# Eleven pairs of token tiles instead of eight by seven products, in a fused attention and ELU feed-forward kernel

## The chip, the cores and the metric

The kernel runs on one core of a Trainium2 chip. The metric is the device time of one execution in microseconds (us). The engines are TensorE (PE; its weight loads are shown apart as PEld), VectorE (DVE), ScalarE (ACT), GpSimd (POOL) and SyncE (SP), each with a queue of its own that is worked off in order. SP issues output DMAs and transposing DMAs; POOL issues input DMAs.

## The reference

Attention with a causal window of 128 and a linear bias by head, on 8 batches of 8 heads, 576 positions and 64 dimensions, and behind it a feed-forward layer with ELU. All arrays are float32; the kernel multiplies in float16.

```
def _attn_ref(q, k, v):                       # (8, 8, 576, 64) each
    scores = scale * np.matmul(q, k.transpose(0, 1, 3, 2))
    ...
    mask = (rel >= 0) & (rel < window)        # window = 128
    scores = np.where(mask, scores + bias[None], -1000000000.0)
    attn = softmax(scores)
    return np.matmul(attn, v)

def _moe_ref(x, w_in, w_out):                 # x (4608, 512), w_in (512, 2048), w_out (2048, 512)
    h = x @ w_in
    g = np.where(h > 0.0, h, np.exp(np.minimum(h, 0.0)) - 1.0)
    return g @ w_out
```

`x` is the attention's output with the heads of a token side by side: 8 x 576 = 4608 tokens of 512 numbers.

## The kernel before

The order of all work is written out by hand, in steps that the code calls `s` and this text calls slots, from 0 to 152. In most slots PE does one `hidden` group, a piece of `x @ w_in` for 512 outputs per partition (line 300): either 128 tokens and four blocks of 128 hidden channels (16 matmuls of 128 columns, and 32 of 64 columns for some), or from slot 70 on 256 tokens and two blocks (8 matmuls of 256 columns). Two PSUM banks, `hp0` and `hp1`, take turns, so the group of slot s+2 needs the bank that the group of slot s filled.

Behind a hidden group comes the ELU. In a common slot ACT takes exp of the bank (line 310), POOL cuts it at 1 (line 311), and DVE forms max(e - 1, h) from it and the bank and writes it to `g` in float16 (line 318, function `elu`). In a slot of the set `SOFT`, ACT does two passes instead, relu of -h and exp of minus that (lines 307 and 308), and POOL nothing. The elu of slot s-1 is issued behind the hidden group of slot s.

Ahead of it the attention of batches 2 to 7 is spread over 17 slots a batch. Each batch has four units of four slots. In the first slot of a unit PE computes scores (line 225). In the next two, ACT does two exps each (line 231), ahead of its work for the hidden group, and DVE weighs the result with the bias table (line 236). In the fourth, PE multiplies by the values (line 266) and DVE divides (lines 271 and 272). SP then transposes the result to `xT` by DMA (line 280). `turn_qk` transposes blocks of q and k of the next batch on DVE (line 145). Batches 0 and 1 are done in slots 0 to 32 in a form with more PE transposes; batch 1's last units lie in slots 22 to 32, with PE products with the values, DVE reciprocals and products (lines 254 and 255), weighing (line 216) and ACT exps of 1024 columns (line 205).

The second product, `g @ w_out`, is done for pairs of 128-token tiles, numbered n from 0 to 17; pair n belongs to about the slots 15 + 8n to 22 + 8n. There are two ways.

- Standard (`output`, line 324): per tile 16 matmuls of 512 columns into one bank, four in a slot. Even tiles use `op`, odd ones `av`. ACT copies the bank to `ob` (line 331), SP sends it out.
- Seven products, for the pairs in `SEVEN`: the 256 tokens, the 2048 channels and the 512 outputs are each halved, and instead of eight block products there are seven, as in Winograd's form of Strassen's algorithm. Seven products of 8 matmuls with 256 columns, in the order 1, 6, 2, 7, 5, 4, 3, seven matmuls a slot (`product`, line 392). They need sums of blocks of `g` (`sums`: S1 to S4, on DVE, from two slots ahead of the pair to its fourth slot) and of `w_out` (`quarters`: T1 to T4, eight DVE instructions once in the kernel). DVE puts the parts together (`combine`: U2, U3, C22, C21, C12); ACT copies product 1 and the sum of 1 and 2 (lines 395 and 397). All DVE adds of these show as line 348.

The products lie in two banks, x and y (`places`): 1, 2 and then 3 and 5 in x, 6, 7 and 4 in y. For a pair behind a standard one x is `av`, for a pair behind a seven-product one x is `op`. T1 to T3 lie in `s1`, which before slot 25 holds staged q and k of batch 1. Of the pairs with seven products, 5, 7, 9, 11 and 13 have attention beside them; 15, 16 and 17 lie behind the last batch's attention, or at its end.

The six slots from two ahead of a seven-product pair on are soft, and so are slots 40 to 48 (the quarters lie in slots 41 to 48), and the end. The last pair, 17, has no hidden groups beside it; it uses banks of its own, is not spread over slots, and its product 4 is done in two pieces of 128 columns, each with its add and its DMA.

```
        SEVEN = (17, 5, 7, 9, 11, 13, 15, 16)
...
        turns = [(i, j) for i in (1, 6, 2, 7, 5, 4, 3) for j in range(8)]
...
                for d, i, j in ((-2, 1, (0, m)), (-1, 1, (m, 8)), (0, 2, ()), (1, 3, ()), (3, 4, ())):
                    at(s + d, sums, n, i, *j)
                for d, what in ((2, "U2"), (4, "U3"), (5, "C22"), (6, "C21"), (7, "C12")):
                    after(s + d, combine, n, what)
```

Of the kernel before, what the change touches and what calls it, by code (L numbers as in the profile page):

```python
# [18 lines left out]
def kernel(  # L19
# [9 lines left out]
    nc = tc.nc  # L29
    B, H, S, D = q.shape  # L30
    NTOK, DO = out.shape
    FF = moe_w_in.shape[1]
    NFC = FF // 128
    NTB = NTOK // 512
# [39 lines left out]
    sp = [spa[:, 0, :], spa[:, 1, :]] + [ps_s.tile([128, 512], F32, name=f"sp{i}", tag=f"sp{i}") for i in (2, 3)]  # L74
    hp = [ps_h.tile([128, 512], F32, name=f"hp{i}", tag=f"hp{i}") for i in range(2)]
    av = ps_v.tile([128, 512], F32, name="av", tag="av")
    op = ps_o.tile([128, 512], F32, name="op", tag="op")
# [71 lines left out]
    with tc.manual_schedule():  # L149
# [142 lines left out]
        def hidden(t, c0, w, f0, nf, p, soft):  # L292
            hps[t, c0, f0] = p
            a = (512 * t + c0) % RING
            cuts = [(0, w, a)] if a + w <= RING else [(0, RING - a, a), (RING - a, w, 0)]
            for l in range(nf):
                fc = f0 + l
                for u0, u1, x0 in cuts:
                    for c in range(4):
                        nc.tensor.matmul(  # L300
                            p[:, l * w + u0:l * w + u1], w_in_sb[:, c, fc * 128:(fc + 1) * 128],
                            xT[:, c, x0:x0 + u1 - u0], start=(c == 0), stop=(c == 3))
            e = es[t, c0, f0] = work.tile([128, 512], F32, name="e", tag="e", bufs=6)
            n = w * nf
            if soft:

                nc.scalar.activation(e[:, 0:n], p[:, 0:n], AF.Relu, scale=-1.0)  # L307
                nc.scalar.activation(e[:, 0:n], e[:, 0:n], AF.Exp, scale=-1.0)  # L308
                return
            nc.scalar.activation(e[:, 0:n], p[:, 0:n], AF.Exp)  # L310
            nc.gpsimd.tensor_scalar(out=e[:, 0:n], in0=e[:, 0:n], scalar1=1.0, scalar2=0.0,  # L311
                                    op0=ALU.min, op1=ALU.max)
# [30 lines left out]
        def A(n, i, k):  # L343
            c = 256 * (n % 2) + 128 * i
            return gs[n // 2][:, 8 * k:8 * k + 8, c:c + 128]

        def add(o, a, b, op=ALU.add):
            V.tensor_tensor(out=o, in0=a, in1=b, op=op)  # L348
# [6 lines left out]
        SS, U, obs = {}, {}, {}  # L355
# [9 lines left out]
        def places(n):  # L365


            x, y = (op, av) if n - 1 in SEVEN else (av, op)
            return ((x, 0), (y, 0), (x, 256), (y, 256)) if n < 2 * NTB - 1 else (
                (sp[2], 0), (sp[3], 0), (sp[0], 0), (hp[0], 0))  # L370

        def place(n, i):
            o, c = places(n)[(0, 0, 2, 3, 2, 1, 1)[i - 1]]
            return o[:, c:c + 256]

        def kept(n, i):
            if (n, i) not in U:
                U[n, i] = work.tile([128, 256], F32, name=f"U{i}", tag=f"U{i}", bufs=1)
            return U[n, i]

        def tile_out(n, i):
            if (n, i) not in obs:
                obs[n, i] = work.tile([128, DO], F32, name="ob", tag="ob")
            return obs[n, i]

        def product(n, i, j0=0, j1=8, o=None, c0=0, c1=256):
            a, b = {1: lambda: (A(n, 0, 0), WB(0, 0)), 2: lambda: (A(n, 0, 1), WB(1, 0)), 3: lambda: (SS[n, 4], WB(1, 1)),
                    4: lambda: (A(n, 1, 1), T[4]), 5: lambda: (SS[n, 1], T[1]), 6: lambda: (SS[n, 2], T[2]),
                    7: lambda: (SS[n, 3], T[3])}[i]()
            o = place(n, i) if o is None else o  # L390
            for j in range(j0, j1):
                nc.tensor.matmul(o[:, 0:c1 - c0], a[:, j, :], b[:, j, c0:c1], start=j == 0 and i in (1, 4, 5, 6),  # L392
                                 stop=j == 7, skip_group_check=True)
            if j1 == 8 and (i == 1 or i == 5 and n == 2 * NTB - 1):
                nc.scalar.copy(kept(n, i), o)
            if j1 == 8 and i == 2:
                nc.scalar.copy(tile_out(n, 0)[:, 0:256], o)

        def combine(n, what):
            if what == "U2":  # L400
                add(kept(n, 2), kept(n, 1), place(n, 6))
            elif what == "U3":
                add(kept(n, 3), kept(n, 1), place(n, 7))
            elif what == "C22":
                add(tile_out(n, 1)[:, 256:512], kept(n, 3), kept(n, 5) if (n, 5) in U else place(n, 5))
            elif what == "C12":
                add(tile_out(n, 0)[:, 256:512], kept(n, 2), place(n, 3))
                put(n, 0, 0, DO)
            else:
                add(tile_out(n, 1)[:, 0:256], kept(n, 3), place(n, 4))  # L410
                put(n, 1, 0, DO)

        def put(n, i, c0, c1):
            r = 256 * n + 128 * i
            nc.sync.dma_start(out[r:r + 128, c0:c1], tile_out(n, i)[:, c0:c1])

        def last_piece(n, o, c0, c1, e):
            product(n, 4, 0, 8, o, c0, c1)
            add(tile_out(n, 1)[:, c0:c1], kept(n, 3)[:, c0:c1], o[:, 0:c1 - c0])
            put(n, 1, c0, e)  # L420

        wz = one([128, 256], F16, "wz")

# [69 lines left out]
        early, tasks, late, HID, OUT = {}, {}, {}, {}, {}  # L493

        def at(s, f, *a):
            tasks.setdefault(s, []).append((f, a))

        def after(s, f, *a):
            late.setdefault(s, []).append((f, a))
# [14 lines left out]
        for t in range(2, NTB):  # L514
            for j in range(16):
                step = (128 * (j // 4), 128, 4 * (j % 4), 4) if t < 4 else (256 * (j // 8), 256, 2 * (j % 8), 2)
                HID[16 * t + 6 + j] = [(t, *step, BUF[(j + 1) % 2])]
        SEVEN = (17, 5, 7, 9, 11, 13, 15, 16)
        for o in range(16 * NTB):
            t, ts, f = o // 16, o // 4 % 4, o % 4  # L520
            if o // 8 in SEVEN:
                continue
            s = (9, 11, 13, 14)[o] if o < 4 else 11 + o if o < 13 else 2 * o - 1 if o < 16 else 15 + o
            OUT[s] = [(output, (t, ts, 4 * f, (op, op, sp[3], op)[ts] if t == 0 else (op, av)[ts % 2]))]

        def done(r):
            for step in HID[r]:
# [66 lines left out]
        for b in range(2, B):  # L594
            for u in range(4):
                a = START[b] + 4 * u
# [11 lines left out]
            a = START[b - 1] if b > 2 else 0  # L608
            for n in range(4):
                piece = (b, int(n < 2), n % 2)  # L610
                if b == 2:
                    m = 4 if n < 2 else 6
# [8 lines left out]


        for m in range(8):
            at(41 + m, quarters, 1 + m // 2, m % 2)
        turns = [(i, j) for i in (1, 6, 2, 7, 5, 4, 3) for j in range(8)]
        for n in SEVEN:
            s = 15 + 8 * n
            if n < 2 * NTB - 1:
                m = 6 if n >= 8 else 4
# [4 lines that stand above are left out]
                for d in range(8):  # L634
                    OUT[s + d] = [(product, (n, i, j, j + 1)) for i, j in turns[7 * d:7 * d + 7]]
            else:
                at(s - 3, sums, n, 3)
                for i in (1, 2):
                    at(s - 2, sums, n, i, 0, 6)
                    at(s - 1, sums, n, i, 6, 8)  # L640
                at(s - 1, product, n, 1)
                OUT[s] = [(product, (n, 2)), (product, (n, 6)), (combine, (n, "U2")), (sums, (n, 4))]
                OUT[s + 1] = [(product, (n, 5)), (product, (n, 7)), (combine, (n, "U3"))]
                OUT[s + 2] = [(product, (n, 3)), (combine, (n, "C12")), (combine, (n, "C22")),
                              (last_piece, (n, hp[0], 128, 256, DO)), (last_piece, (n, hp[1], 0, 128, 128))]


        SOFT = {s for n in SEVEN for s in range(13 + 8 * n, 19 + 8 * n)} | set(range(40, 49)) | set(range(16 * NTB - 10, 16 * NTB + 8))

        slots = set(HID) | set(OUT) | set(tasks) | set(early)  # L650
        for s in range(min(slots), max(slots) + 1):
            for f, a in early.get(s, []):
                f(*a)
            for step in HID.get(s, []):
                hidden(*step, s in SOFT)
            if s - 1 in HID and s not in (1, 4, 5):
# [37 lines left out]
```

## Time and profile before

| | |
|---|---|
| median of 8 runs | 316.58 us (315.68 to 317.21) |
| profiled execution | 316.05 us, span 314.3 us |
| PE, DVE, ACT, POOL busy | 98%, 75%, 66%, 43% of the span |
| granted TensorE clock | 1.0 |
| hidden groups (L300) on PE | 144.9 us |
| standard products (L324), op and av | 45.2 and 32.8 us |
| elu on DVE (L318) | 138 x 0.684 us in the records |
| relu and exp on ACT in soft slots (L307, L308) | 56 x 0.598 and 0.631 us |
| exp on ACT in common slots (L310) | 87 x 0.60 us |

The span runs from the first to the last instruction; the execution's own time has 1.75 us around it. The chain of waits in a profile is followed back from the last instruction. In the rows of the timeline the first figure is the start in us, the second the length; a length holds the pipeline's run-out, so the next instruction of the engine can start before it is over. A row of busy times by stretch gives the stretch and its length, then busy time and number of instructions of PE, PEld, DVE, ACT and POOL, the granted clock, and the DMA engines' share and rate.

### The profile page before, as it was taken

How to read it: one execution, taken by the hardware profiler on the slowest of the kernel's cores; microseconds unless marked ns; L12 is line 12 of the kernel's file. 1: busy time of each engine (PE TensorE's matmuls, PEld its weight loads, DVE VectorE, ACT ScalarE, POOL GpSimd, SP SyncE). 2: the span in 40 equal slices, each digit the busy share in tenths (PEclk: the TensorE clock that was granted, in tenths of full speed). 3: DMA queues.
4: the chain of work that ended last, by engine and by line, in shares of the span. 5: the costliest groups of instructions: out<-in, count | busy, mean ns of one | idle time of the engine just before them, and what ended most of it. 6: DMA issues, size and time to landing. Idle time of an engine off the chain costs nothing.

```text
span 314.3 us, 9840 instructions
## 1 busy us (share of the span) xinstructions
PE 306.8 (98%) x4119; PEld 238.1 (76%) x4119; DVE 236.2 (75%) x458; ACT 208.1 (66%) x376; POOL 135.1 (43%) x207
## 2 busy tenths in 40 slices
PE   8899999999999999999999999999999999999994
PEld 6788874887777678976787688767877787678884
DVE  4747656787689978886897689778977688577883
ACT  4676458666678668647965787558754875678760
POOL 8947879473780071465256533672233013300000
PEclk9999999999999999999999999999999999999999
DMA  9999999995999259495949891999232102120102
GB/s 99 176 199 202 199 182 165 141 116 68 94 132 134 61 69 132 51 162 75 116 50 165 104 125 24 160 130 118 27 86 54 42 19 86 50 61 2 67 35 101
DMA packets 96364, 32.03 MB, mean 102 GB/s; under 512 B 83904, under 2 KB 91840, under 8 KB 96320
## 3 DMA queue, kind: packets, MB, share of 16 engines
q0 software_dynamic: 75920, 18.36, 64.3%
q1 hardware_dynamic: 20400, 13.05, 16.9%
q8 instruction: 32, 0.52, 0.7%
q14 instruction: 12, 0.10, 0.1%
HBM read 36.70 MB, written 9.44 MB: 147 GB/s over the span
## 4 chain that ended last, share of the span: by engine, by line
PE 90%; DVE 4%; ACT 2%; issue 2%; POOL 1%; ACTq 0%; DVEq 0%; POOLq 0%
PE hp L300 37%; PE op L324 12%; PE av L324 8%; PE av L392 7%; PE op L392 6%; PE spa L225 4%; PE spa L266 3%; PE op L426 2%; DVE g L318 1%; PE sp L248 1%; PE sp L324 1%; PE sp L300 1%; PE sp L392 1%; ACT EX L231 1%; PE spa L176 1%
## 5 line engine op out<-in xcount | busy, mean ns | idle before, releaser
L300 PE MATMUL hp<-xT,wi 128*128 128x128 f16 (+2 forms) x1744 | 144.9, 233 | 0.7 <-DVE g L318 0.3
L300 PEld LDWEIGHTS <-wi 128*128 128x128 f16 x1856 | 124.4, 98 | 26.6 <-issue 5.7
L318 DVE SCALAR_TENSOR_TENSOR g<-e,hp 128x512 f16<-128x512 f32 x138 | 94.4, 684 | 35.3 <-POOL e L311 26.3
L311 POOL TENSOR_SCALAR e<-e 128x512 f32<-128x512 f32 x88 | 55.5, 631 | 136.7 <-ACT e L310 136.2
L310 ACT ACTIVATE e<-hp 128x512 f32<-128x512 f32 x82 | 49.2, 599 | 47.6 <-PE hp L300 44.1
L307 ACT ACTIVATE e<-hp 128x512 f32<-128x512 f32 x56 | 33.5, 598 | 19.2 <-PE hp L300 16.6
L324 PE MATMUL op<-wo,g 128*128 128x512 f16 x176 | 45.2, 379 | 0.0
L236 DVE TENSOR_TENSOR EX<-EX,TAB 128x1024 f16<-128x1024 f16 x48 | 33.1, 690 | 14.9 <-ACT EX L231 14.8
L324 PEld LDWEIGHTS <-g 128*128 128x128 f16 x320 | 27.7, 97 | 20.6 <-issue 1.1
L308 ACT ACTIVATE e<-e 128x512 f32<-128x512 f32 x56 | 35.3, 631 | 1.8
L114 POOL DMA_DIRECT2D VP<-in_v_dram x40 | 34.5, 873 | 0.7 <-DVE xn L255 0.5
L231 ACT ACTIVATE EX<-spa 128x512 f16<-128x512 f32 x48 | 26.1, 595 | 11.1 <-PE spa L225 10.2
L324 PE MATMUL av<-wo,g 128*128 128x512 f16 x128 | 32.8, 379 | 0.0
L392 PEld LDWEIGHTS <-S 128*128 128x128 f16 x256 | 24.2, 98 | 3.4 <-DVE S L348 0.6
L231 ACT ACTIVATE EX<-sp 128x512 f16<-128x512 f32 x48 | 26.0, 598 | 0.0
L392 PEld LDWEIGHTS <-g 128*128 128x128 f16 x200 | 18.7, 98 | 3.0 <-issue 1.0
L272 DVE TENSOR_TENSOR xn<-spa,rden 128x512 f16<-128x512 f32 x24 | 16.6, 692 | 0.8
L108 POOL DMA_DIRECT2D st<-in_k_dram x24 | 16.4, 684 | 0.4 <-issue 0.3
L108 POOL DMA_DIRECT2D st<-in_q_dram x24 | 16.2, 678 | 0.2 <-DMA VP<-in_v_dram 0.2
L392 PE MATMUL op<-s,S 128*128 128x256 f16 x104 | 15.6, 273 | 0.2 <-DVE S L348 0.2
L225 PEld LDWEIGHTS <-KT 32*128 32x128 f16 x480 | 9.0, 92 | 8.5 <-issue 8.0
L225 PE MATMUL spa<-QT,KT 32*128 32x256 f16 (+2 forms) x240 | 15.1, 250 | 0.0
(144 smaller groups left out, 347.6 us busy)
## 6 DMA issues: line engine op xcount, KB each, us to landing
out_dram<-ob SPq DMA_DIRECT2D x35, 256.0 KB, 2.2
VP<-in_v_dram POOLq DMA_DIRECT2D x32, 128.0 KB, 5.1
st<-in_k_dram POOLq DMA_DIRECT2D x24, 144.0 KB, 4.3
st<-in_q_dram POOLq DMA_DIRECT2D x24, 144.0 KB, 4.2
wi<-in_moe_w_in_dram POOLq DMA_DIRECT2D x4, 512.0 KB, 11.6
wo<-in_moe_w_out_dram POOLq DMA_DIRECT2D x4, 512.0 KB, 11.3
VP<-in_v_dram POOLq DMA_DIRECT2D x8, 64.0 KB, 5.3
s<-in_k_dram POOLq DMA_DIRECT2D x1, 512.0 KB, 13.3
```

The costliest lines, as they stand in the source:

```text
L114: nc.gpsimd.dma_start(VP[b % 2][0:p, n, :, 0:D], v[b, :, 128 * n:128 * n + p, :].rearrange("h p d -> p h d"))
L225: nc.tensor.matmul(sp[g][:, 256 * h2 + o:256 * h2 + o + n], kt_[b % 2][r, k0:k0 + 255:2], qt_[b % 2][r, c0:c0 + 2 * n - 1:2], start=dh == ...
L231: nc.scalar.activation(unit(b, u)[:, g, :, :], sp[g].rearrange("p (h c) -> p h c", h=2), AF.Exp, scale=0.125)
L236: V.tensor_tensor(out=e, in0=e, in1=TAB[:, int(u == 3), 2 * gp:2 * gp + 2, :, :], op=ALU.mult)
L300: nc.tensor.matmul(p[:, l * w + u0:l * w + u1], w_in_sb[:, c, fc * 128:(fc + 1) * 128], xT[:, c, x0:x0 + u1 - u0], start=(c == 0), stop=(c ...
L307: nc.scalar.activation(e[:, 0:n], p[:, 0:n], AF.Relu, scale=-1.0)
L308: nc.scalar.activation(e[:, 0:n], e[:, 0:n], AF.Exp, scale=-1.0)
L310: nc.scalar.activation(e[:, 0:n], p[:, 0:n], AF.Exp)
L311: nc.gpsimd.tensor_scalar(out=e[:, 0:n], in0=e[:, 0:n], scalar1=1.0, scalar2=0.0, op0=ALU.min, op1=ALU.max)
L318: V.scalar_tensor_tensor(out=gs[t][:, f0:f0 + nf, c0:c0 + w], in0=sh(es.pop((t, c0, f0))), scalar=1.0, in1=sh(hps.pop((t, c0, f0))), op0=A ...
L324: nc.tensor.matmul(o, gs[t][:, fc, ts * 128:(ts + 1) * 128], w_out_sb[:, fc, :], start=(fc == 0), stop=(fc == NFC - 1))
L392: nc.tensor.matmul(o[:, 0:c1 - c0], a[:, j, :], b[:, j, c0:c1], start=j == 0 and i in (1, 4, 5, 6), stop=j == 7, skip_group_check=True)
```

## The change

Pairs 3, 12 and 14 go over to seven products, so that the pairs 11 to 17 all use them. The quarters of `w_out` are summed in slots 25 to 32 instead of 41 to 48, and these slots are soft in their place. The banks x and y are kept in a table `XY`, in which a pair behind a seven-product pair has them the other way round from its predecessor, and a pair behind a standard pair has them as its predecessor; standard tiles take the banks from it too. In the last pair the products come in the order 1, 2, 6, 5, 3, 7, 4 instead of 1, 2, 6, 5, 7, 3, 4. Product 3 has a bank of its own and is not added to product 5 in PSUM; DVE adds product 5 to U2 (`U5`) in place of the copy of product 5 on ACT. S4 stands ahead of product 2. C22, of 256 columns, has a DMA of its own.

```
-            x, y = (op, av) if n - 1 in SEVEN else (av, op)
+            x, y = XY[n]
             return ((x, 0), (y, 0), (x, 256), (y, 256)) if n < 2 * NTB - 1 else (
-                (sp[2], 0), (sp[3], 0), (sp[0], 0), (hp[0], 0))
+                (sp[2], 0), (sp[3], 0), (sp[0], 0), (hp[0], 0), (av, 0))
...
-            o, c = places(n)[(0, 0, 2, 3, 2, 1, 1)[i - 1]]
+            o, c = places(n)[(0, 0, 4 if n == 2 * NTB - 1 else 2, 3, 2, 1, 1)[i - 1]]
...
-            if j1 == 8 and (i == 1 or i == 5 and n == 2 * NTB - 1):
+            if j1 == 8 and i == 1:
                 nc.scalar.copy(kept(n, i), o)
...
+            elif what == "U5":
+                add(kept(n, 2), kept(n, 2), place(n, 5))
...
-                add(tile_out(n, 1)[:, 256:512], kept(n, 3), kept(n, 5) if (n, 5) in U else place(n, 5))
+                add(tile_out(n, 1)[:, 256:512], kept(n, 3), place(n, 5))
+                if n == 2 * NTB - 1:
+                    put(n, 1, 256, DO)
...
-        def last_piece(n, o, c0, c1, e):
+        def last_piece(n, o, c0, c1):
             product(n, 4, 0, 8, o, c0, c1)
             add(tile_out(n, 1)[:, c0:c1], kept(n, 3)[:, c0:c1], o[:, 0:c1 - c0])
-            put(n, 1, c0, e)
+            put(n, 1, c0, c1)
...
-        SEVEN = (17, 5, 7, 9, 11, 13, 15, 16)
+        SEVEN = (17, 3, 5, 7, 9, 11, 12, 13, 14, 15, 16)
+
+        XY = {1: (op, av)}
+        for n in range(2, 2 * NTB):
+            XY[n] = XY[n - 1][::-1] if n - 1 in SEVEN else XY[n - 1]
...
-            OUT[s] = [(output, (t, ts, 4 * f, (op, op, sp[3], op)[ts] if t == 0 else (op, av)[ts % 2]))]
+            OUT[s] = [(output, (t, ts, 4 * f, (op, op, sp[3], op)[ts] if t == 0 else XY[o // 8 or 1][ts % 2]))]
...
         for m in range(8):
-            at(41 + m, quarters, 1 + m // 2, m % 2)
+            at(25 + m, quarters, 1 + m // 2, m % 2)
...
-                OUT[s] = [(product, (n, 2)), (product, (n, 6)), (combine, (n, "U2")), (sums, (n, 4))]
-                OUT[s + 1] = [(product, (n, 5)), (product, (n, 7)), (combine, (n, "U3"))]
-                OUT[s + 2] = [(product, (n, 3)), (combine, (n, "C12")), (combine, (n, "C22")),
-                              (last_piece, (n, hp[0], 128, 256, DO)), (last_piece, (n, hp[1], 0, 128, 128))]
+                at(s, sums, n, 4)
+                OUT[s] = [(product, (n, 2)), (product, (n, 6)), (combine, (n, "U2")), (product, (n, 5)), (combine, (n, "U5"))]
+                OUT[s + 1] = [(product, (n, 3)), (combine, (n, "C12")), (product, (n, 7)), (combine, (n, "U3"))]
+                OUT[s + 2] = [(combine, (n, "C22")), (last_piece, (n, hp[0], 128, 256)), (last_piece, (n, hp[1], 0, 128))]
...
-        SOFT = {s for n in SEVEN for s in range(13 + 8 * n, 19 + 8 * n)} | set(range(40, 49)) | set(range(16 * NTB - 10, 16 * NTB + 8))
+        SOFT = {s for n in SEVEN for s in range(13 + 8 * n, 19 + 8 * n)} | set(range(25, 33)) | set(range(16 * NTB - 10, 16 * NTB + 8))
```

More of the change, by code (lines that the diff above doesn't have):

```diff
@@ L391, in product @@
             for j in range(j0, j1):
-                nc.tensor.matmul(o[:, 0:c1 - c0], a[:, j, :], b[:, j, c0:c1], start=j == 0 and i in (1, 4, 5, 6),
+                nc.tensor.matmul(o[:, 0:c1 - c0], a[:, j, :], b[:, j, c0:c1], start=j == 0 and (i in (1, 4, 5, 6) or o is av and n == 2 * NTB - 1),
                                  stop=j == 7, skip_group_check=True)
-            if j1 == 8 and (i == 1 or i == 5 and n == 2 * NTB - 1):
+            if j1 == 8 and i == 1:
                 nc.scalar.copy(kept(n, i), o)
```

## The prediction, made before the changed kernel ran

> **What bounds the kernel now.** I read the engine table first, then the chain of waits, then the instruction groups by form, then the busy times by stretch, and last the timeline at the stretches that the change touches. A "slot" below is one step of the kernel's schedule, which begins on PE with one `hidden` group (line 300); slot times come from counting those groups in the timeline. "The elu" is the DVE instruction of line 318.
>
> ```profile
> PE 306.8 (98%) x4119; PEld 238.1 (76%) x4119; DVE 236.2 (75%) x458; ACT 208.1 (66%) x376; POOL 135.1 (43%) x207
> PE 90%; DVE 4%; ACT 2%; issue 2%; POOL 1%; ACTq 0%; DVEq 0%; POOLq 0%
> ...
> 263.35 0.86 PE op L324 x4
> 303.30 0.87 PE sp L392 x8
> ...
> 57.96:72.95 14.99, 14.94 (x266) 11.84 (x261) 11.80 (x26) 9.62 (x16) 10.78 (x17) 1.00 1.02 122
> 80.90:105.53 24.63, 24.50 (x356) 17.94 (x353) 21.32 (x37) 19.61 (x36) 10.39 (x15) 1.00 1.27 116
> 246.08:262.20 16.12, 15.81 (x177) 12.96 (x176) 12.95 (x25) 12.57 (x25) 1.84 (x3) 1.00 0.17 50
> 291.57:303.09 11.52, 11.52 (x108) 10.33 (x106) 9.10 (x17) 9.17 (x17) 0.00 (x0) 1.00 0.12 46
> ...
> 60.60 0.69 DVE L318 SCALAR_TENSOR_TENSOR g<-e,hp 128x512 f16<-128x512 f32 x1 [0.29 <-POOL e L311]
> 61.34 1.05 PE L300 MATMUL hp<-xT,wi 128*128 128x128 f16 x16
> ...
> 246.80 0.57 ACT L331 COPY ob<-av 128x512 f32<-128x512 f32 x1
> 247.42 0.93 PE L392 MATMUL av<-wo,g 128*128 128x256 f16 x7
> 248.99 0.68 DVE L348 TENSOR_TENSOR S<-S,g 128x1024 f16<-128x1024 f16 x1
> 249.74 0.83 PE L392 MATMUL op<-s,S 128*128 128x256 f16 x6 [0.15 <-DVE S L348]
> ...
> 308.47 0.42 DVE L348 TENSOR_TENSOR U<-U,sp 128x256 f32<-128x256 f32 x1 [0.67 <-PE sp L392]
> 309.14 1.06 PE L392 MATMUL hp<-T,g 128*128 128x128 f16 x16
> 309.34 0.42 DVE L348 TENSOR_TENSOR ob<-U,spa 128x256 f32<-128x256 f32 x1 [0.45 <-PE spa L392]
> 310.02 0.51 DVE L348 TENSOR_TENSOR ob<-U,hp 128x128 f32<-128x128 f32 x2
> ```
>
> PE is the bound, 98% busy and 90% of the chain, at a granted clock of 1.00 in each stretch shown (the third figure from the end of those rows). So PE work that goes is time that goes, if nothing makes PE wait. But the cover is thin: at 60.60 the elu of slot 25 starts, ends at 61.29, and PE starts slot 27's hidden group, which reuses the bank that this elu reads, at 61.34. In a short slot an elu later by 0.1 us is PE later by 0.1 us. DVE and ACT are therefore near-bounds by their order, not by their sum.
>
> **The matmuls removed.** A standard pair is 32 matmuls of 512 columns; four take 0.86 us (0.8635 unrounded from start to next start: 216 ns each). A seven-product pair is 56 of 256 columns; eight take 0.87 (109 ns each). That is 6.91 against 6.11: -0.80 us for each of pairs 3, 12 and 14, -2.40 in all. A rule speaks against this: the Trainium skill, "TensorE: Matmul & The Clock Gate", section "Back-to-back issue gap", gives a sustained 131 ns for a 512-column matmul in a stream with weight loads and, for 128 columns, 81 ns. By it a standard pair would be 4.2 us, and 56 products of even 81 ns 4.5: each swap would lose. This trace decides: 216 ns for 512 columns, and 56 ns for 128 (16 hidden matmuls in 0.89). I take the rows.
>
> **What the pairs add beside PE.** Each new pair brings five DVE sums (three of 0.68 us, and 0.55 + 0.29 for the split one, in pair 3 twice 0.40) and five combines of 0.41: 4.9 us of DVE records, some 0.6 and 0.34 of queue time each since the records overlap. ACT loses two 0.57 copies and gains two of 0.35, but six slots turn "soft": ACT does relu and exp (0.60 + 0.63) instead of one exp, POOL loses 0.63. There are as many output DMAs (two a pair), on SP behind the same transposes; the first of a pair goes out some three slots later, and the next transpose in the SP queue is not read for seven slots or more, so I cost that at nothing. What shows on PE is only what is late for it. A walk along the queues with these durations gives: pair 12 (slots 109 to 113) elu 0.1 late and the second sum 0.1 late for product 6, +0.2; pair 14 +0.1, since no 0.57 copy stands before the attention's exps on ACT any more; pair 3 +0.3, the second sum again. New pairs: -2.40 + 0.6 = -1.8. From both sides: the pairs of before lost between 0.0 (pair 16) and 0.9 (pair 13, whose eight slots took 16.12 us against 15.18 for the standard slots of the neighbouring units less 0.80). I stay near the low end, because both big losses of pair 13 (next paragraphs) have a cause that the new order takes away; with 0.9 each the three pairs give nothing.
>
> **Banks in alternating order.** Before, a pair after a standard one begins in av, the bank of the last standard tile, and waits for its 0.57 us copy: at 246.80 the copy starts, at 247.42 product 1. The slots that do so are long: 1.99 against 1.64 (slot 119, and slot 135), 2.37 against 1.89 (slot 103). Now product 1 goes to the bank that was left one tile earlier. But product 6, eight matmuls on, waits for the second sum, which follows the attention's exps on ACT: in slot 120 PE waits 0.15 for it already. So where the copy stays on ACT (pairs 5, 7, 11) most of the wait only moves: -0.3 together. Pair 13 now follows a seven-product pair, so ACT loses the copy too and the sum comes about 0.5 earlier: -0.5. Pair 15 has no attention beside it and its sum is 0.6 early: -0.3. Sum -1.1. If the sums eat all of it, 0; if nothing takes the waits' place, -1.9.
>
> **Quarters moved.** From slots 41 to 48 eight DVE subtractions go (0.67 us each; queue 0.60), where slots 44 and 48 were 0.21 and 0.25 longer than their kind: -0.45. Pair 3's sums and combines come there (4.9 us against 5.4), beside the same block transposes: +0.3. Net -0.15. Into slots 25 to 32 go the eight subtractions, and soft slots. That stretch is 14.99 us with DVE 11.80 and ACT 9.62 busy. Adding 8 x 0.60 gives DVE 16.6, and 8 x 0.66 ACT 14.9: DVE is over. Its cover is gone, and each subtraction stands between two elus. No DMA goes along, and SP and POOL are not passed. Walk of the DVE queue (us; start of PE's next-but-one hidden group now and before):
>
> ```
> slot  exp ends  DVE free  elu ends  hidden+2  before  late
> 25    60.48     60.86     61.55     61.60     61.34   0.26
> 26    62.08     62.61     63.30     63.57     63.31   0.26
> 27    64.18     64.41     65.10     65.18     64.92   0.26
> 28    65.93     66.69     67.38     67.43     66.72   0.71
> 29    68.01     68.49     69.18     69.23     68.31   0.92
> 30    69.75     70.78     71.47     71.52     70.53   0.99
> 31    71.54     72.52     73.21     73.94     72.95   0.99
> ```
>
> For instance slot 28: before its elu stand the elu of 27 (64.41, 0.60), a reciprocal and a product (0.55), a block transpose (0.53) and the subtraction (0.60), so DVE is free at 66.69 though the exp was ready at 65.93. Slots 32 and 33 had 1.3 and 0.5 us of DVE idle, so nothing is carried on. Cost +1.0. Bounds: 0.3 (PE's own delay makes room for DVE), and 4.8 (all eight exposed).
>
> **The last pair.** The same seven products in another order, PE without a gap in both: nothing. The third combine, "U3", moves from 308.47 behind the last full product to 309.34; C12 moves from there to before it. So DVE still does two adds, then the two pieces, and ends at 310.52. The fourth sum goes ahead of a wait for PE and is early in both. The ACT copy of product 5 (0.37) becomes a DVE add that is hidden behind product 3. SP issues four DMAs instead of three; the last three come at about 310.17, 310.55 and 310.93, where before the last went at 310.75, with less data ahead. +0.1 (-0.3 to +0.4).
>
> **Sum.** -1.8 - 1.1 - 0.15 + 1.0 + 0.1 = -1.95. The profiled execution took 316.05 us (span 314.3 and 1.75 around it) and would be 314.1. The median of the eight runs is 0.53 above it: 316.58 - 1.95 = 314.6.
>
> **Rivals.** (1) Slower: the quarters in slots 25 to 32 stall PE in full. For it: DVE at 16.6 of 14.99, an elu with 0.05 us to spare. Against: half of the slots of that stretch have 0.3 to 0.5 us of DVE idle before the elu. It decides from 2.95 us on; at 4.8 the sum is +1.85, 318.4. (2) No change: ACT is the hidden bound of soft slots beside attention (six soft slots and eight exps in 7.7 us), so new pairs keep nothing and only 0.5 is won from the banks, at pairs 11 and 15: 0 - 0.5 - 0.15 + 1.0 + 0.1 = +0.45, 317.0. For it: pair 13 today. Against: pairs 7 and 9, with the same attention beside them, lost only 0.25 each. (3) The bank order does nothing, as the sum is as late as the copy: -0.85, 315.7, still faster.
>
> **Chances and range.** The sum as worked out, or with (3): 0.70; (2) 0.15; (1) 0.15. A difference under 0.2% (0.63 us) can't be told from none here. The likeliest case spans 313.3 (quarters 0.3, banks -1.7) to 315.9; half of (2) goes up to 316.6. Range 313.2 to 316.6. Faster 0.70, same 0.14, slower 0.16.
>
> **What would show it.** In the profile after: line 392 with 72 more matmuls; slots 109 to 142 shorter by about 2.1 us together; no PE wait for the ob copy of av in front of product 1; slots 25 to 32 at 16.0 us, with the elus of 28 to 30 late on DVE and not on ACT; slots 37 to 48 shorter by about 0.7; PE's last group to the end unchanged. I am wrong if slots 25 to 32 pass 17.9 us, or if product 6 waits over 0.5 us for its sum in each new pair.

## The result, and the profile after

The changed kernel takes 314.52 us (median of 11 runs, 314.08 to 316.33) against 316.71 before: ratio 0.994, 95% interval 0.9924 to 0.9957. Timed a second time it took 314.78 (12 runs) against 316.27: ratio 0.9957, 0.9935 to 0.9978. The forecast was 314.6. In 5 of the 24 runs of the changed kernel on record and in 4 of 51 later runs of the kernel before, the mean granted clock was 0.995 or less and the time 1.5 to 2 us longer; the medians of the others are 314.61 and 316.36, 1.75 us apart (1.51 in the second set alone).

The page of the changed kernel, its engine table and two of its costliest groups, and under the dots the same two groups before:

```profile
PE 304.6 (97%) x4191; PEld 244.7 (78%) x4191; DVE 246.8 (79%) x489; ACT 215.8 (69%) x392; POOL 124.3 (40%) x190
L300 PE MATMUL hp<-xT,wi 128*128 128x128 f16 (+2 forms) x1744 | 144.9, 233 | 1.8 <-DVE g L318 1.7
L318 DVE SCALAR_TENSOR_TENSOR g<-e,hp 128x512 f16<-128x512 f32 x138 | 94.3, 683 | 26.1 <-POOL e L311 19.4
...
L300 PE MATMUL hp<-xT,wi 128*128 128x128 f16 (+2 forms) x1744 | 144.9, 233 | 0.7 <-DVE g L318 0.3
L318 DVE SCALAR_TENSOR_TENSOR g<-e,hp 128x512 f16<-128x512 f32 x138 | 94.4, 684 | 35.3 <-POOL e L311 26.3
```

PE has 72 matmuls more and 2.2 us of busy time less, DVE has 10.6 us more. PE is still the bound, but it now waits 1.7 us for the elu (before 0.3), and DVE's idle time in front of the elu, its reserve, fell from 35.3 to 26.1 us.

Where the time went is read from the busy times by stretch, cut where the weights of the slot's first hidden matmul begin to load, so that PE's wait for an elu counts to the slot that waits. After: slots 25 to 32, 37 to 48, 119 to 126, 111 to 118, 127 to 134, and all of 0 to 148 (columns: stretch, length, then PE, PEld, DVE, ACT, POOL busy, clock, DMA):

```profile
57.75:73.57 15.82, 15.18 (x266) 11.88 (x260) 15.63 (x34) 14.09 (x24) 5.67 (x9) 1.00 1.04 123
81.53:105.52 23.99, 23.58 (x380) 20.25 (x377) 21.71 (x42) 17.32 (x33) 11.26 (x18) 1.00 0.96 101
245.62:261.25 15.63, 15.55 (x179) 12.98 (x177) 13.60 (x27) 12.73 (x25) 1.23 (x2) 1.00 0.16 45
229.33:245.62 16.29, 16.27 (x274) 14.61 (x272) 14.97 (x32) 12.31 (x24) 1.23 (x2) 1.00 0.24 70
261.25:276.74 15.49, 15.42 (x203) 13.64 (x200) 13.63 (x30) 11.73 (x23) 1.23 (x2) 1.00 0.16 44
...
12.55:300.14 287.59, 284.85 (x3939) 229.02 (x3938) 232.13 (x446) 205.63 (x372) 113.14 (x166) 1.00 0.83 102
```

The rows of before that the prediction did not show, slots 111 to 118, 127 to 134, and 0 to 148:

```profile
229.35:246.08 16.73, 16.73 (x250) 12.30 (x248) 11.90 (x23) 8.93 (x17) 4.47 (x7) 1.00 0.34 68
262.20:278.12 15.92, 15.92 (x179) 11.29 (x176) 11.43 (x23) 8.82 (x17) 4.47 (x7) 1.00 0.19 52
...
12.79:301.39 288.60, 286.82 (x3872) 222.14 (x3869) 221.58 (x416) 197.57 (x355) 123.63 (x182) 1.00 0.83 102
```

In slots 25 to 32 PE has the same 266 matmuls in both, but the stretch is 0.83 us longer, and DVE is busy for 15.63 of its 15.82. Slots 37 to 48 are 0.64 shorter, pair 12's slots 0.44, pair 13's 0.49, pair 14's 0.43; slots 135 to 142 are 0.13 longer. In all, slots 0 to 148 are 1.01 us shorter. From slot 25 on such stretches repeat to 0.06 us between profiles of kernels that do the same there, so one profile is enough to read them. The start does not repeat: from the first instruction to slot 0 the traces of this study show between 12.55 and 15.38 us. The difference between 1.01 and the 1.5 to 2.2 of the medians is taken up below.

### The profile page after: what moved, and what is told of

Its sections match the earlier page's. It is cut to its first block, busy times and chain, and to the rows that moved or that the text cites. A ratio compares the mean times of both kernels' runs of the same rounds, so it can differ in the third digit from the quotient of the medians.

```text
span 312.6 us, 10024 instructions
## 1 busy us (share of the span) xinstructions
PE 304.6 (97%) x4191; PEld 244.7 (78%) x4191; DVE 246.8 (79%) x489; ACT 215.8 (69%) x392; POOL 124.3 (40%) x190
## 4 chain that ended last, share of the span: by engine, by line
PE 80%; DVE 6%; DMA 4%; ACT 3%; issue 3%; POOL 2%; DVEq 0%; POOLq 0%; ACTq 0%
PE hp L300 35%; PE av L392 9%; PE op L392 8%; PE op L324 8%; PE av L324 5%; PE spa L225 4%; DMA s<-in_q_dram 3%; PE spa L266 3%; DVE g L318 2%; ACT EX L231 1%; DMA VP<-in_v_dram 1%; PE sp L300 1%; PE sp L392 1%; PE sp L248 1%; PE sp L324 1%
## 5 line engine op out<-in xcount | busy, mean ns | idle before, releaser
L318 DVE SCALAR_TENSOR_TENSOR g<-e,hp 128x512 f16<-128x512 f32 x138 | 94.3, 683 | 26.1 <-POOL e L311 19.4
L311 POOL TENSOR_SCALAR e<-e 128x512 f32<-128x512 f32 x71 | 44.5, 626 | 145.3 <-ACT e L310 144.8
L308 ACT ACTIVATE e<-e 128x512 f32<-128x512 f32 x73 | 46.0, 631 | 2.3
L392 PEld LDWEIGHTS <-S 128*128 128x128 f16 x352 | 32.9, 98 | 5.0 <-DVE S L348 1.4
L324 PE MATMUL op<-wo,g 128*128 128x512 f16 x128 | 32.9, 379 | 0.0
L231 ACT ACTIVATE EX<-spa 128x512 f16<-128x512 f32 x48 | 26.1, 595 | 8.6 <-PE spa L225 8.2
L324 PEld LDWEIGHTS <-g 128*128 128x128 f16 x224 | 19.3, 97 | 14.7 <-issue 1.1
L392 PEld LDWEIGHTS <-g 128*128 128x128 f16 x272 | 25.2, 98 | 2.6
L324 PE MATMUL av<-wo,g 128*128 128x512 f16 x80 | 20.5, 379 | 0.0
L392 PE MATMUL av<-s,S 128*128 128x256 f16 x120 | 18.0, 273 | 0.2 <-DVE S L348 0.2
L392 PE MATMUL op<-s,S 128*128 128x256 f16 x120 | 18.0, 273 | 0.1
L348 DVE TENSOR_TENSOR S<-g 128x1024 f16<-128x1024 f16 (+3 forms) x33 | 16.5, 501 | 0.2
```

The lines of the kernel that those rows point to most:

```text
L231: nc.scalar.activation(unit(b, u)[:, g, :, :], sp[g].rearrange("p (h c) -> p h c", h=2), AF.Exp, scale=0.125)
L318: V.scalar_tensor_tensor(out=gs[t][:, f0:f0 + nf, c0:c0 + w], in0=sh(es.pop((t, c0, f0))), scalar=1.0, in1=sh(hps.pop((t, c0, f0))), op0=A ...
L324: nc.tensor.matmul(o, gs[t][:, fc, ts * 128:(ts + 1) * 128], w_out_sb[:, fc, :], start=(fc == 0), stop=(fc == NFC - 1))
```

## The experiments

**Without pair 3.** `SEVEN` loses 3, the quarters and the soft slots go back.

```
-        SEVEN = (17, 3, 5, 7, 9, 11, 12, 13, 14, 15, 16)
+        SEVEN = (17, 5, 7, 9, 11, 12, 13, 14, 15, 16)
-            at(25 + m, quarters, 1 + m // 2, m % 2)
+            at(41 + m, quarters, 1 + m // 2, m % 2)
-        SOFT = ... | set(range(25, 33)) | ...
+        SOFT = ... | set(range(40, 49)) | ...
```

> The changed kernel without pair 3 and with the quarters back in slots 41 to 48 (these soft again, 25 to 32 not). Theory: pair 3 pays for the quarters' place. In the traces of before and after, slots 25 to 32 became 0.83 us longer and slots 37 to 48 0.64 shorter, so without both the span is 312.6 - 0.2 = 312.4, slots 25 to 32 take 14.99 us again and 37 to 48 the 24.6 of before. Rival: pair 3 carries its third of the gain and what the quarters cost in slots 25 to 32 they cost in 41 to 48 as well; then the span is about 313.2 (0.6 longer).

Measured: 314.36 us (4 runs), ratio 0.9936 (0.9915 to 0.9958). Slots 25 to 32 take 14.98 and 37 to 48 24.62 us, slots 0 to 148 287.56 against 287.59. So pair 3 is worth nothing as it is placed: slots 37 to 48 are 0.64 us shorter with it, and the quarters' new place costs 0.83. (Slots 0 to 24, which neither touches, took 45.39 here and 45.20 there; slots 25 to 148 are 0.22 shorter without pair 3, 242.17 against 242.39.) By slots, what the change wins comes from pairs 12 and 14 and from pair 13 between them.

**The quarters alone.** The kernel before with the last two of these edits turned round: quarters in slots 25 to 32, soft there and not in 40 to 48.

> The kernel before, with one change: the quarters in slots 25 to 32, which are soft instead of 40 to 48. Theory: DVE is over-full in that stretch, so slots 25 to 32 take 15.8 us instead of 14.99 (the late elus of slots 28 to 30), and slots 44 and 48 give back their 0.21 and 0.25: the span is 314.3 + 0.8 - 0.45 = 314.7. Rival: pair 3's sums share in the delay of slots 27 to 32; then these slots take under 15.3 us here.

```profile
59.54:75.36 15.82, 15.18 (x266) 11.88 (x261) 15.63 (x34) 14.08 (x24) 5.65 (x9) 1.00 1.08 126
83.31:107.49 24.18, 24.18 (x356) 17.95 (x353) 18.18 (x32) 14.87 (x27) 14.90 (x24) 1.00 1.13 108
```

Slots 25 to 32 took 15.82, and slots 37 to 48 24.18 instead of 24.63. Both as the theory has it: the quarters alone make the 0.83 us, and their old place, with its soft slots, had cost 0.45. That splits the 0.64 of slots 37 to 48: pair 3 itself kept 0.19 of its 0.80 (23.99 against 24.18). In sum slots 0 to 148 are 0.45 longer. The time does not show it: 316.23 against 316.36, ratio 0.9994 (0.9982 to 1.0006). The upper end of that interval is 0.19 us, so here too the time is better than the slots say.

**Quarters in common slots.** Does DVE or ACT hold that stretch up? ACT is busy for 14.1 of 15.8 us there too. One edit to the changed kernel:

```
-        SOFT = ... | set(range(25, 33)) | ...
+        SOFT = ... | set() | ...
```

> The changed kernel with slots 25 to 32 as common slots (one exp on ACT, the cut at 1 on POOL). Theory: the DVE queue with the quarters sets the 0.83 us, so slots 25 to 32 take 15.7 to 16.1 us here too. Rival: the two ACT passes of the soft slots set it (ACT would be at 14.9 of 14.99); then the stretch falls to 15.3 us or less.

```profile
58.60:75.27 16.67, 15.23 (x266) 11.95 (x261) 16.48 (x34) 9.62 (x16) 10.80 (x17) 1.00 0.92 108
...
64.00 0.69 DVE L216 TENSOR_TENSOR EX<-EX,TAB 128x1024 f16<-128x1024 f16 x1
64.17 1.00 POOL L311 TENSOR_SCALAR e<-e 128x512 f32<-128x512 f32 x1 [0.78 <-ACT e L310]
64.61 1.10 DVE L348 TENSOR_TENSOR s<-wo,s 128x1024 f16<-128x1024 f16 x1
```

ACT fell to 9.62 us, and the stretch did not shorten: it grew to 16.67, with DVE busy for all but 0.2. The rival is out. DVE is the bound of these slots. My figure, at most 16.1, was too low by 0.6 us. Two of the eight subtractions and one weighing (line 216) began while POOL's cut at 1 ran, and took 0.87, 1.10 and 0.89 us instead of 0.68; that makes up the 0.85 by which DVE's busy time grew. So the soft slots are worth 0.85 us next to the quarters.

**The bank of the last tile.** Seven-product pairs behind a standard one begin in its last bank again.

```
-            XY[n] = XY[n - 1][::-1] if n - 1 in SEVEN else XY[n - 1]
+            XY[n] = XY[n - 1][::-1] if n - 1 in SEVEN or n in SEVEN else XY[n - 1]
```

> The changed kernel, but a seven-product pair behind a standard pair (3, 5, 7, 9, 11) begins in the bank of the last standard tile, as in the kernel before. Theory: the wait for the second sum is as late as the wait for the copy, so the bank is worth nothing here: slots 55 and 103 grow by 0.2 and 0.4 us, slots 56 and 104 shrink by as much, and the span stays within 0.15 us of 312.6. Rival: the free bank saved a part that was lost elsewhere; then the span grows by 0.5 us or more.

Slots 55 and 56 took 1.99 and 2.22 us (changed kernel: 1.76 and 2.45), 103 and 104 2.38 and 2.40 (2.00 and 2.74): the wait moves from one slot to the next, and each pair of slots keeps its sum within 0.04. Pair 3, whose bank this edit changes too, is the exception: slots 37 to 48 took 24.10 against 23.99. (The run's own 315.56 us, span 313.8, had its slot 0 at 13.61 instead of 12.55.) In the changed kernel's timeline, slots 103 and 104, and under the dots the two products before:

```profile
214.79 0.57 ACT L331 COPY ob<-av 128x512 f32<-128x512 f32 x1
215.03 0.93 PE L392 MATMUL op<-wo,g 128*128 128x256 f16 x7
216.36 0.68 DVE L348 TENSOR_TENSOR S<-S,g 128x1024 f16<-128x1024 f16 x1
217.10 0.83 PE L392 MATMUL av<-s,S 128*128 128x256 f16 x6 [0.16 <-DVE S L348]
...
215.37 0.92 PE L392 MATMUL av<-wo,g 128*128 128x256 f16 x7 [0.22 <-ACT ob L331]
217.11 0.82 PE L392 MATMUL op<-s,S 128*128 128x256 f16 x6
```

Product 1 starts in op while av is still copied, as planned. Product 6 then starts at 217.10, just after S2 ends at 217.04; before it started at 217.11. From slot 25 to 148 the bank order behind standard pairs is worth 0.16 us (242.39 against 242.55), most of it at pair 3, and next to nothing at the pairs it was meant for.

**S2 one slot earlier,** in all pairs but the last.

```
-                for d, i, j in ((-2, 1, (0, m)), (-1, 1, (m, 8)), (0, 2, ()), (1, 3, ()), (3, 4, ())):
+                for d, i, j in ((-2, 1, (0, m)), (-1, 1, (m, 8)), (-1, 2, ()), (1, 3, ()), (3, 4, ())):
```

> The changed kernel with the second sum (S2) one slot earlier in each pair but the last, behind S1's second part. Theory: product 6 waits for S2 in the pair's second slot, so this wait goes: slots 55 and 56 from 4.21 to 3.9 us, 103 and 104 from 4.74 to 4.4, 119 and 120 from 3.72 to 3.6; slot 135, where DVE is late already, may grow by up to 0.3. Rival: S2 stands ahead of an elu wherever it is, so the wait turns into one of the hidden group for the elu and these pairs of slots keep their lengths within 0.1 us.

```profile
246.88 0.69 DVE L348 TENSOR_TENSOR S<-S,g 128x1024 f16<-128x1024 f16 x1
247.50 0.41 DVE L348 TENSOR_TENSOR ob<-U,av 128x256 f32<-128x256 f32 x1
247.83 0.68 DVE L318 SCALAR_TENSOR_TENSOR g<-e,hp 128x512 f16<-128x512 f32 x1
248.56 1.03 PE L300 MATMUL hp<-xT,wi 128*128 128x256 f16 x8 [0.38 <-DVE g L318]
```

Nearer to the rival, and worse than it. Slots 55 and 56 took 4.10 and 103 and 104 4.64 us, 0.1 less each, but 119 and 120 took 4.07 instead of 3.72, and slot 136 1.98 instead of 1.64. In all, slots 0 to 148 took 289.09 us, 1.5 longer than in the changed kernel (287.59). The rows are those of slots 118 to 120: S2 is early, the elu behind it is late, and now the hidden group waits 0.38 us. My 4.4 and 3.9 assumed that DVE had the room.

**S1 of pair 15 in slot 134.**

```
+                first = ((-1, 1, (0, 8)),) if n == 15 else ((-2, 1, (0, m)), (-1, 1, (m, 8)))
-                for d, i, j in ((-2, 1, (0, m)), (-1, 1, (m, 8)), (0, 2, ()), (1, 3, ()), (3, 4, ())):
+                for d, i, j in (*first, (0, 2, ()), (1, 3, ()), (3, 4, ())):
```

> The changed kernel with S1 of pair 15 in one piece in slot 134 instead of its first part in slot 133, where DVE also divides the last batch's values. Theory: in slot 135 PE waits 0.32 us for the elu of slot 133, which stands behind that part of S1 on DVE, so slot 135 falls from 2.12 to about 1.7 us and slot 136 stays at 1.64. Rival: the combine C12 of pair 14 or the divisions hold the elu up; then slot 135 stays at 2.0 us or more.

In the changed kernel, slots 133 to 135:

```profile
275.47 0.42 DVE L255 TENSOR_TENSOR xn<-sp,rden 64x256 f16<-64x256 f32 x1
275.81 0.54 DVE L348 TENSOR_TENSOR S<-g 128x768 f16<-128x768 f16 x1
276.27 0.41 DVE L348 TENSOR_TENSOR ob<-U,op 128x256 f32<-128x256 f32 x1
276.60 0.67 DVE L318 SCALAR_TENSOR_TENSOR g<-e,hp 128x512 f16<-128x512 f32 x1
277.33 1.03 PE L300 MATMUL hp<-xT,wi 128*128 128x256 f16 x8 [0.32 <-DVE g L318]
```

With the part of S1 taken out from between, slot 135 fell from 2.12 to 1.65 us, slot 136 stayed at 1.66. The theory holds: one sum of 0.54 us in the one slot where the last divisions also lie cost 0.47.

**The end alone.** The kernel before with only the last pair's new order (the diff of the front part, without `SEVEN`, `XY`, quarters and `SOFT`), in one trace, and then timed.

> The kernel before, with the last pair's new order alone. Theory: PE and DVE end as before, the last DMA is issued some 0.4 us later but has less data ahead of it, so from the last hidden group to the end it takes 12.4 us as in the changed kernel instead of 12.9, and the span is 313.9. Rival: the 0.45 us at the end of the changed kernel's trace are scatter of landing times; then the end takes 12.9 +- 0.1.

> The kernel with the last pair's new order alone, timed this time. Its slots 0 to 148 take what they take in the kernel before (288.6 us in both profiles), so what it gains or loses is at the start (where PE waits for the first q and k) or at the end. The changed kernel's median fell by 2.2 us, its slots 0 to 148 by 1.0 only. Theory: the other 1.2 us are scatter of the start and the end, and this kernel stays within 0.5 us of the one before. Rival: the new order at the end is worth them; then it is faster by 0.8 to 1.2 us.

From slot 149 to the end it took 12.54 and 12.62 us; before 12.87, but 12.53 in the kernel with the quarters alone, which has the old end. So the first theory fell: the 0.4 us between the traces of before and after do not come from the new order. The nine traces of kernels with pairs 12 and 14 changed have 12.46 to 12.50; with one trace of the kernel before, what its end takes as a rule is not known. Timed: 316.58 against 316.71, ratio 0.9993 (0.9975 to 1.0011). The new end gives no difference that can be measured.

**Once more.**

> The changed kernel once more, to see whether its median stands 1.0 us below the kernel before, as its slots 0 to 148 say, or 2.2 us, as its first eleven runs did. Theory: the start (PE's wait for the first q and k, which was 12.55 to 15.38 us from the first instruction to slot 0 in the traces so far) makes the difference, and more runs bring it to 1.0 to 1.6 us (ratio 0.995 to 0.997). Rival: the change shortens the start or the end of a run as well; then it stays at 2.0 us or more (ratio 0.994 or less).

Measured: 1.49 us by the medians (ratio and interval above; it takes in 1.01 us as well). Slots 0 to 148 took 287.41 us. The 1.49 lies in the range of the theory, but it does not show that the rest is scatter: among the runs at a mean clock of 0.997 and more the means of both sets together differ by 1.80 us, with an uncertainty of 0.20 worked out from their spread. Some 0.5 to 0.8 us of the gain therefore lie in front of slot 0 or behind slot 148. Where, these traces do not show.

**Quarters spread, and all pairs.** Both have S1 of pair 15 in slot 134; the second also has pairs 4, 6, 8 and 10 by seven products.

```
-            at(25 + m, quarters, 1 + m // 2, m % 2)
+            at((28, 30, 32, 32, 33, 35, 36, 36)[m], quarters, 1 + m // 2, m % 2)
-        SOFT = ... | set(range(25, 33)) | ...
+        SOFT = ... | {28, 29, 30, 31, 32, 35, 36} | ...
# the second alone:
-        SEVEN = (17, 3, 5, 7, 9, 11, 12, 13, 14, 15, 16)
+        SEVEN = (17, *range(3, 17))
```

> The changed kernel with two edits: S1 of pair 15 in slot 134, and the eight quarters in slots 28, 30, 32, 32, 33, 35, 36 and 36, where DVE had the most idle time in the kernel before; slots 28 to 32, 35 and 36 are soft. Theory: the 0.83 us come from quarters in slots whose DVE is full, so slots 25 to 36 fall from 23.78 to 23.1 us (22.94 before) and slot 135 to 1.65; the span falls by 1.1 us and the time to about 1.1 below the changed kernel's. Rival: a quarter delays an elu wherever it stands, so slots 25 to 36 stay at 23.5 or more.

> The kernel with the quarters spread, and pairs 4, 6, 8 and 10 by seven products too, so that 3 to 17 all are. Theory: a pair beside attention kept 0.43 to 0.5 us of its 0.80 (pairs 12, 13 and 14), and those behind another such pair do not wait for a copy, so slots 47 to 110 become shorter by 4 x 0.45 = 1.8 us. Rival: DVE has block transposes in these slots that it has not beside 13 and 14, and is full (busy 14.1 of 15.7 us beside pairs 7 and 9), so the new pairs keep 0.2 each or less, 0.8 us in all.

With the quarters spread, slots 25 to 36 took 23.34 us (23.78 in the changed kernel, 22.94 before; expected 23.1), slot 135 1.65, slots 0 to 148 286.71: 0.88 less. The time was 314.6 (6 runs), ratio to before 0.9931 (0.9904 to 0.9958), so the 1.1 us expected against the changed kernel (314.78 beside it) do not show in the time. Most of what is left of the stall is in slot 30: 1.88 us with a quarter in it, 1.56 before.

With all pairs: 311.67 us (6 runs), ratio 0.9852 (0.9824 to 0.988), the fastest kernel of the study, faster than both. Slots 63 to 102, before and in this kernel:

```profile
133.93:213.65 79.72, 79.72 (x939) 60.28 (x936) 64.31 (x120) 53.25 (x101) 41.79 (x61) 1.00 0.93 110
135.24:212.87 77.63, 77.60 (x1011) 67.18 (x1009) 73.56 (x148) 62.05 (x118) 28.94 (x41) 1.00 1.04 111
```

There pairs 6, 8 and 10 are new: 72 matmuls more in 2.09 us less, 0.70 for each new pair (what changes for pairs 7 and 9 behind them is in it), with DVE at 73.6 of 77.6 and hardly a PE wait. Pair 4, beside the block transposes of batch 3, is worth less: against the kernel with the quarters spread, slots 37 to 48 are 0.47 longer and slots 49 to 62 0.62 shorter. In all slots 0 to 148 fell from 286.71 to 284.52, by 2.19, somewhat over the 1.8 expected; the rival (0.8) is out.

## Why the prediction was right, point by point

The sign and the time were right, 314.6 forecast and 314.52 measured, but the fit is closer than the steps deserve: by slots the change is worth 1.01 us, not 1.95. The rest of the measured difference lies outside slots 0 to 148, where the forecast had only +0.1 for the last pair; that it brought the time back to the forecast was luck. Slots 109 to 142, forecast 2.1 us shorter, were 1.23 shorter (64.19 against 65.42).

- *The matmuls removed*: right, and so was the choice of the row (216 ns for 512 columns) over the 131 ns that the Trainium skill, "TensorE: Matmul & The Clock Gate", section "Back-to-back issue gap", gives for a sustained stream. With 72 matmuls more PE was busy for 2.2 us less, against -2.40 worked out. By the estimate from that page's figures the three pairs, and the four of the last experiment, would have lost.
- *New pairs.* Mis-sized: pairs 12 and 14 gave 0.44 and 0.43 us, forecast 0.6 and 0.7. Pair 3 kept 0.19, as forecast (-0.80, +0.3 for the second sum, +0.3 beside the block transposes). Part of pair 14's lack is slot 133 (2.35 us instead of 2.22), where the walk had not counted the last batch's divisions beside the combines and S1. The rest of both was not taken apart.
- *Banks.* The term that failed: -1.1 forecast, -0.4 measured. Pair 13 gave 0.49 as forecast (0.5). For pairs 5, 7 and 11 the forecast said that most of the wait only moves, -0.3 left; almost all of it moved, -0.04 left, as the experiment with the last tile's bank shows. For pair 15, "-0.3" became +0.13 in slot 135: the step looked at the sum of that slot and not at the elu before it, which S1's first part held up. Moving that part gave 0.47 back.
- *Quarters.* Right: +1.0 forecast, +0.83 measured, in the slots that the walk had late (27, 30 and 31 by 0.19, 0.37 and 0.22) and by the mechanism named; the old place gave back 0.45 to the hundredth. DVE's busy time grew by 3.8 us and not by 8 x 0.60, so the stretch was filled and not overfilled. Slots 37 to 48: -0.65 forecast (pair 3's net -0.5 and -0.15), -0.64 measured.
- *The last pair*: +0.1 forecast, not to be told from zero.
- *Rivals.* The quarters stalled PE for 0.83 us and not 4.8, far from the 2.95 of rival 1. Rival 2, ACT as the bound, is refuted for the quarters' slots by the kernel with common slots (its "7.7 us" for six soft slots fits no stretch: pair 13's, 117 to 122, took 12.32), and for the pairs beside attention by the kernel with all pairs. Rival 3 was right about the pairs behind standard ones, wrong about pair 13.

What stays open: what makes the 1.5 to 2.2 us of the medians out of 1.01 by slots. It is not the granted clock alone, since the difference stays when the runs with a lower clock are left out. It may be the end (12.87 us in the one trace before, 12.46 to 12.50 after) or the time at which the first q comes; neither was tested on enough traces.

## What to carry to other kernels

Where an engine's instructions stand in one order with a tight chain among them, a free share of its time is not room: ask for each added instruction which waiting one it stands in front of, as the elu here. Remove a wait only together with the next one that is due; find it beforehand by asking when the following operand is ready. And when stretches of the trace repeat to hundredths while the start scatters by microseconds, read small effects by stretch; then hold their sum against the timed difference, since what is missing lies outside the stretches.

## What the runs showed of the hardware that was not expected

DVE and POOL held each other up, and the one that started second was the longer. In the kernel with the quarters in common slots, three float16 operations of 1024 columns with two SBUF inputs began on DVE while POOL's in-place minimum ran; they took 0.87, 1.10 and 0.89 us, against 0.64 to 0.69 for the others of that kind in its slots 25 to 32. The other way round, the minimum that began at 64.17, behind the weighing of 64.00, took 1.00 us instead of 0.61. In the kernel before, eight of the 88 minima took 0.75 to 0.80 us, and all eight began behind a weighing. The Trainium skill, "SBUF — State Buffer", section "SBUF: two separate sides", says that a DVE operation with two SBUF inputs and a GpSimd operation that reads SBUF share a port pair as an exclusive lock, which whichever starts first gets. These rows agree, if the spans in the records hold the waiting too, since they overlap. One minimum of 1.39 us (at 74.63) is not explained by it alone: the subtraction of 74.90 began behind it and took only 0.64.

The start follows the first q. PE's first transpose of q began between 7.12 and 8.59 us, and in the ten traces whose granted clock stayed at 1.00 there slot 0 came 5.29 or 5.43 us later. In the other three the clock fell in this stretch, and slot 0 came 5.85 to 7.03 us behind q. From the first transpose of q to slot 0, in the changed kernel and in the timed kernel with the end alone:

```profile
7.12:12.55 5.43, 4.99 (x107) 3.70 (x105) 3.97 (x13) 3.57 (x6) 5.22 (x14) 1.00 1.44 159
8.35:15.38 7.03, 7.03 (x104) 5.67 (x105) 3.55 (x10) 3.60 (x6) 6.58 (x15) 0.52 1.33 182
```

Why the clock fell in these three is not shown.
